# Moving eight rotations, four weight sums and one load within the second block's projection

## The chip, the cores and the metric

The kernel runs on one core of a Trainium2 chip. The metric is the device time in microseconds of one execution, and smaller is better. The profile is one execution of the same program, recorded instruction by instruction. The engines are TensorE (PE, matrix products), VectorE (DVE), ScalarE (ACT), GpSimd (POOL, which here mostly issues DMAs) and SyncE (SP, which issues DMAs only). Each engine works through its own list of instructions in the order in which the program appended them; between engines there are only semaphores.

## The reference

The input x has 2048 rows of 1024 features. Three things are added: x itself, a diagonal state-space layer, and a dense layer, both of the normalised x.

```python
xn = _layernorm(x)
# state-space layer (complex, diagonal, 1024 states)
Lam_bar = exp(dt * Lam);  B_bar = ((Lam_bar - 1) / Lam)[:, None] * Bmat
Bu = einsum("bld,pd->blp", xn, B_bar)
h[t] = Lam_bar * h[t-1] + Bu[t]                     # over 2048 steps
y = 2 * (h @ Cmat.T).real + xn * Dskip
# dense layer, 1024 -> 3584 -> 1024
z = xn @ w1 + b1
return x + y + (z * tanh(softplus(z))) @ w2
```

The result is 2048 x 1024 in bf16.

## The kernel before, in words

**Blocks.** The 2048 rows are worked through in four blocks of 512, blk 0 to 3 in the code. `FAST` is 1, so the code's special cases for `blk == FAST` are those of the second block, and `SPLIT` holds blk 2 and 3. A block has these stages on PE: the dense layer's first product (line 818 in blk 0 and 1), the projection of x by B (line 882), the dense layer's second product and the output product of the states by C (both line 1193, accumulated in the same eight PSUM banks), and then four additions on DVE that put x and the sum together (line 1262, `finish`), each with a store issued by ACT (line 1254).

**The projection.** From blk 1 on the product of x and B isn't made with eight partial products but with seven (a scheme after Strassen), numbered 1 to 7. `project_fast` walks through a written list, `WHOLE` for blk 1, in which each word is one step. The letters a, b, c, d are the four pairs of state tiles, and the digit is the product (`a2`, `c4`). Behind each product `evacuate` copies a bank to SBUF on DVE or ACT (lines 897, 899, 924, 926) or joins it with an earlier copy on DVE (line 907). Products of one pair follow each other in the same banks, so a product may have to wait for a join or a copy: product 4 takes the bank that the join of product 7 reads, for example. The other words are `r` (rotate one state tile by its phase: four DVE operations, lines 848 to 853), `u` (`open_unit`: six matmuls that begin the second dense product in one bank), `v` (`w_scale`: ACT scales a weight group in place, line 1087, and POOL stores three parts of it), `n` (`w_load`: POOL loads a raw weight group in four DMAs, line 1026) and `k0` (take one step from the list `steps` and do it).

**The weight groups.** In blk 2 and 3 the dense layer's first product is made by the same scheme, with letters p, q, s, w, x, y, z. That needs scaled weights and sums of them, prepared once in DRAM (`wsd`) for the seven groups 0 to 6. For one group: load the raw weights into half of the buffer `hb` or into `act`; find their size (for groups 0 to 2: `w_abs`, line 1037 on ACT; `w_row`, two small DMAs `wmd` and `wmx` on POOL; `w_exponent`, lines 1071 to 1078 on DVE); scale; store; then `w_sums`, which puts four steps on the list, each one DVE operation (line 1102) and one POOL store of 256 KB (line 1081). Groups 3, 5 and 0 use the lower half of `hb`, groups 4, 6 and 1 the upper half, group 2 uses `act` 0 to 7. So group 1 can be loaded only when the stores of group 6's sums have left the upper half.

**Order in the second block.** The list of steps for group 5 is made at the last tile of the first dense product, and `WHOLE` takes them with four `k0` between its products. Rotations r0 and r1 stand among the joins of pairs c and d. Behind `project_fast`, ACT takes statistics of the next block's x (`next_stats`) and measures group 0, and the list for group 6 is made. Then the recurrences follow on DVE (`recur`, one state tile each: two scans, line 1158, and four operations). Behind recurrence 0 and 1 two steps of group 6 each are done, then POOL loads group 1, and behind it group 2. Behind recurrence 7 DVE works out the exponents of groups 0 to 2, and ACT scales them. Then DVE adds the skip term to the next block's x (lines 563, 565), forms the differences of x that the fast scheme needs (line 1378), carries the state over, and makes the four output additions. The next block's x is turned by four DMA transposes on SP (line 569).

**Weights on the way.** SP loads all streamed weights into a ring of seven slots (lines 410 and 413), in the order of use, each as soon as its slot has been read.

Of the kernel before, what the change touches and what calls it, by code (L numbers as in the profile page):

```python
# [163 lines left out]
def build_kernel(nc, A_x, A_Lambda_re, A_Lambda_im, A_B_re, A_B_im, A_C_re, A_C_im,  # L164
# [16 lines left out]
    FAST = 1  # L181
    NPL = 12
    SPLIT = range(2, NB)
    GROUPS = ((0, 7), (7, NPL), (NPL, NPL + 8), (NPL + 8, NF))
    HEAD = "a2 a1 b2 b1 a5 b5 a6 b6 a3 b3 a7 b7 c2 d2 a4 b4 c5 c1 r0 d5 d1 r1 c6 c3 d6"
    HEAD1 = "v5 n6 " + HEAD.replace("a4 b4 c5 c1 r0 d5 d1 r1", "a4 b4 k0 c5 c1 k0 r0 d5 d1 k0 r1 k0")
    WHOLE = HEAD1 + " v6 d3 c7 d7 u7 c4 r2 u5 d4 u6 u4 r3 n0 r4 r5 r6 r7"
    LATE = (" a3 b3 a7 b7 c2 d2 a4 b4 c5 c1 d5 d1 c6 c3 d6"
            " d3 c7 w1 d7 w5 w2 c4 d4 w6 r0 x1 x5 x2 w7 w3 r1 x6 w4 y1 y5 y2 x7 x3 r2 y6 x4"
            " z1 z5 g2 z2 y7 y3 z6 y4 u0 z7 u2 z3 u1 z4 u7 g3 r3 r4 r5 r6 r7")  # L190
# [150 lines left out]
    def early(name, shape, dtype, where):  # L341
        b_early.append(Buf(name))
        return nc.alloc_sbuf_tensor_at(name, shape, dtype, offset=base_c + where), b_early[-1]
# [9 lines left out]
    ncs, _ = early("ncs", [P, NR], f32, 10752)  # L353
# [675 lines left out]
    def w_half(i, ci):  # L1029
        kind, t = w_raw(i, ci, 0)  # L1030
        v, b_v = (hb, b_hbf) if kind == "h" else (act, b_actf)
        return v[:, t:t + 4, :].rearrange("p f t -> p (f t)"), b_v[t:t + 4]
# [51 lines left out]
    def w_scale(i):  # L1084
        for ci in range(2):
            t, b_t = w_half(i, ci)
            aop(lambda e, t=t: e.activation(t, t, AF.Copy, scale=wsm(2, i, i + 1)),  # L1087
                reads=b_t + [b_wsm[2][i]], writes=b_t)
        for n, ci, kh in ((1, 0, 0), (2, 0, 1), (4, 1, 1)):
            w_store(i, n, *w_unit(w_raw(i, ci, kh)))  # L1090

    steps = []
# [16 lines left out]
    def project_fast(blk, order, open_unit):  # L1109
        keep = {}  # L1110
        split = order is not WHOLE
        for o in order.split():
            kind, n = o[0], int(o[1:])
            if kind == "r":
                rotate_in(n)
            elif kind == "u":
                open_unit(n)
            elif kind == "g":
                mish(blk, n)
            elif kind == "k":  # L1120
                if steps:
                    steps.pop(0)()
            elif kind == "n":
                w_load(n)
            elif kind == "v":
                w_scale(n)
            elif kind in QUADS:
                w_product(blk, QUADS.index(kind), n)
                w_evacuate(blk, QUADS.index(kind), n, keep)
            else:  # L1130
                product("abcd".index(kind), n)
                evacuate("abcd".index(kind), n, keep, split or kind in "ab")
# [257 lines left out]
    for blk in range(NB):  # L1390

        def side(f):
            if blk:
                at = (8, 10, 12, 15)
                if f in at:
                    ln_skip(blk, at.index(f))
                    if blk >= FAST:
                        sums_x(at.index(f))
                if blk == FAST:
                    if f == 1:  # L1400
                        rows_spread(1)
                    if f == 0:
                        scale_B(0, (1,))
                    if f < 3:
                        scale_B(f + 1)
                    if f in (3, 4, 17, 19):
                        sums_B((3, 4, 17, 19).index(f))
                    if f in (2, 14):
                        w_scale((2, 14).index(f) + 3)
                    if f in (6, 8, 10, 12):  # L1410
                        rows_C(f // 2 + 1)
                    if f == 12:
                        snaps_ready()
                    if f in (10, 19):
                        w_sums((10, 19).index(f) + 3)
                    if f == 15:
                        w_load(5)
                    if f == 27:
                        w_sums(5, True)
                return  # L1420
            if f == 2:
                turn_sines()
            if f == NR:
                aop(lambda e: e.activation(act[:, 0:NR, 0:2 * P], hraw[:, 0:NR, :], AF.Mish),
                    reads=b_hbf[0:4], writes=b_actf[0:NR])
            if f in (19, 27):
                for j in range(4):
                    table(j + (4 if f > 19 else 0))
            if f in (5, 6, 7, 8):
                coefficients(f - 5)  # L1430
            if f in (8, 9, 11, 12):
                ln_skip(0, (8, 9, 11, 12).index(f))
            if f in turns:
                transpose_B(turns.index(f))
            if f >= 26:
                transpose_C(f - 26)
            if f >= 4 * ROWS[0][0] and f % 4 < 2:
                w_most(f // 4, f % 4)
            if f in (23, 25, 26, 27):
                ln_stats_only(1, (23, 25, 26, 27).index(f))  # L1440
            if f == 26:
                w_row(0)

        for f in range(0 if blk in SPLIT else NF):
            first_tile(blk, f)
            side(f)

        near = 0 < blk < NB - 1
        out_stage = tail(blk, n_item[0] + (len(W_ITEMS) if blk in SPLIT else 0))
        open_unit = next(out_stage)  # L1450
        if blk in SPLIT:
            if near:
                for q in range(NQ):
                    load_x(PO, blk + 1, q)
            project_fast(blk, STEPS if near else SEVEN, open_unit)
        elif blk:
            project_fast(blk, WHOLE, open_unit)
        else:
            project_in()
        if near and blk not in SPLIT:  # L1460
            for q in range(NQ):
                next_stats(blk + 1, q)
            w_abs(0)
            w_sums(6, True)
        for j in range(NJ):
            if blk == 0 and j == NJ - 1:
                rows_scale(0)
            recur(blk, j)
            if blk == FAST and j < 2:
                for _ in range(2):  # L1470
                    steps.pop(0)()
                if j == 1:
                    w_load(1)
            if near and j == (5 if blk in SPLIT else 1):
                next_root()
                for q in range(NQ):
                    next_scale(blk + 1, q)
            if blk in SPLIT:
                if j == 1:
                    next(out_stage)  # L1480
                if near and j == 1:
                    for q in range(NQ):
                        next_stats(blk + 1, q)
                if near and j == 5:
                    for q in range(NQ):
                        transpose_dma(q)
                continue
            if blk:
                if j == 1:
                    next(out_stage)  # L1490
                    w_load(2)
                    w_abs(1)
                    w_abs(2)
                    w_row(1)
                if j == 7:
                    w_exponent(1)
                    for i in (0, 1, 2):
                        w_scale(i)
                continue
            if j == 0:  # L1500
                ln_root()
                w_exponent(0)
                for q in range(NQ):
                    ln_scale(1, q)
                next(out_stage)
                for i in range(NHS):
                    rows_load(i)
            scale_C(j)
            for i in {4: (0, 1, 2), 5: (3, 4, 5, 6), 6: (7, 8, 9, 10), 7: range(11, 16)}.get(j, ()):
                rows_size(i)  # L1510
        if near:
            for q in range(NQ):
                ln_skip(blk + 1, q)
            for n in range(4):
                sums_x(n, VE)
        if blk < NB - 1:
            carry()
        if blk == FAST:
            for i in (0, 1, 2):
                w_sums(i, True)  # L1520
        if blk == FAST - 1:
            w_load(3)
            rows_scale(1)
            vop(lambda e: e.tensor_tensor(qi[:], qi[:], c("ss").unsqueeze(1).to_broadcast([P, 2, NJ]), op=ALU.mult),
                reads=[b_qi] + b_ss, writes=[b_qi])
            rows_spread(0)
            scale_B(0, (0,))
            for j in range(4):
                rows_C(j)
            w_load(4)  # L1530
        for _ in out_stage:
            pass
# [36 lines left out]
```

## Time and profile before

| what | value |
|---|---|
| median of 3 runs | 608.08 us (605.46 to 609.31) |
| the profiled execution's own time | 609.85 us |
| its span, first to last instruction | 608.6 us |
| mean granted TensorE clock | 0.997 |
| DVE, ACT, POOL busy | 475.4, 278.5, 122.8 us |
| first dense product and projection of blk 1 | 162 to 210 us, 210 to 238 us |
| last output product of blk 1 ends | 311.8 us |
| the same of blk 2 | 462.8 us |

A line of the profile names the engine, the line of the kernel, what is written and what is read (`ps<-xnT,ring` writes PSUM from x and a ring slot), and the shape. In a timeline the first two numbers are the start and the length in us; `x16` joins sixteen equal instructions, and brackets tell how long the engine sat idle before and what ended that. In the view of waits the numbers are the total, the count and the longest. In the chain each line is a stretch of time and who filled it; the chain is followed back from the last instruction, each time to what released it. Two matmuls of 512 columns start 0.219 us apart at full clock, two of 256 columns 0.109 us; the durations shown are longer, since matmuls overlap. The share of the DMA engines can come out a little over 1.

### The profile page before, as it was taken

What the parts mean: (1) busy time and instruction counts of PE and PEld (TensorE: products, weight loads), DVE (VectorE), ACT (ScalarE), POOL (GpSimd) and SP (SyncE); (2) the same over time, 40 slices, a digit from 0 to 9 for tenths busy, and PEclk for the clock granted to TensorE, in tenths of its full rate; (3) what the DMA queues carried; (4) which work ended last, traced back from release to release, by engine and by line L of the source; (5) the groups of instructions that cost most, each with busy time, mean ns of one, the idle gap of its engine ahead of it and who ended that gap; (6) DMA issues with size and microseconds to landing.
All of it is one profiled execution on the core that took longest, in us unless ns stands there. A gap on an engine that the chain in (4) does not pass through costs nothing.

```text
span 608.6 us, 9262 instructions
## 1 busy us (share of the span) xinstructions
PE 595.7 (98%) x3541; PEld 348.8 (57%) x3583; DVE 475.4 (78%) x748; ACT 278.5 (46%) x367; POOL 122.8 (20%) x162
## 2 busy tenths in 40 slices
PE   8999999999999999999979999999999999999998
PEld 7644444444444585444448888544446888744444
DVE  6998899999789579998186876699943577689923
ACT  4749605489488526834077417470304615620000
POOL 2899200221338333040034100000000000000000
PEclk9999999999999999999989999999999999999999
DMA  9999997992999955699969817554667705764421
GB/s 237 312 236 274 203 195 215 255 356 59 280 357 339 329 179 173 221 236 186 301 247 401 323 53 251 197 193 141 185 193 250 282 6 171 245 207 144 167 71 69
DMA packets 109670, 132.95 MB, mean 218 GB/s; under 512 B 54346, under 2 KB 69322, under 8 KB 109626
## 3 DMA queue, kind: packets, MB, share of 16 engines
q1 hardware_dynamic: 97168, 95.77, 54.4%
q0 software_dynamic: 8768, 28.26, 14.5%
q10 hardware_dynamic: 3690, 8.34, 3.9%
q8 instruction: 28, 0.46, 0.3%
q14 instruction: 16, 0.13, 0.1%
HBM read 99.04 MB, written 21.24 MB: 198 GB/s over the span
## 4 chain that ended last, share of the span: by engine, by line
PE 78%; DVE 9%; DMA 5%; issue 5%; ACT 2%; POOL 1%; SPq 1%; ACTq 0%; DVEq 0%; POOLq 0%
PE ps L1193 37%; PE ps L818 14%; PE ps L952 11%; PE ps L882 10%; PE ps L1139 5%; DMA ring<-in_B_w_dram 2%; DVE mt L848 2%; ACT snaps L972 2%; DMA wmd<-cs 1%; PE ps L638 1%; DVE xx L1262 1%; DVE hT L907 1%; DVE hT L1158 1%; DMA wmx<-wmd 1%; DMA wsd<-hb 1%
## 5 line engine op out<-in xcount | busy, mean ns | idle before, releaser
L1193 PE MATMUL ps<-ring,act 128*128 128x512 bf16 x876 | 194.2, 379 | 2.1 <-DMA ring<-in_B_w_dram 1.1
L1193 PEld LDWEIGHTS ps<-ring,act 128*128 128x128 bf16 x896 | 87.4, 98 | 105.1 <-DMA ring<-in_B_w_dram 2.4
L818 PE MATMUL ps<-xnT,ring 128*128 128x512 bf16 x383 | 84.3, 379 | 0.5
L1193 PE MATMUL ps<-ring,hT 128*128 128x512 bf16 x369 | 81.6, 379 | 0.5
L972 ACT ACTIVATE snaps<-ps,par,cs 128x256 f32<-128x256 f32 x80 | 43.2, 562 | 84.6 <-PE ps L952 49.6
L818 PEld LDWEIGHTS ps<-xnT,ring 128*128 128x128 bf16 x392 | 38.4, 98 | 46.0
L1193 PEld LDWEIGHTS ps<-ring,hT 128*128 128x128 bf16 x378 | 37.0, 98 | 44.6
L1158 DVE TENSOR_TENSOR_SCAN hT<-cs,qi,hT 128x512 bf16<-128x512 f32 x48 | 58.9, 1267 | 0.0
L952 PE MATMUL ps<-TT,ring 128*128 128x256 f16 x448 | 56.6, 275 | 1.0 <-ACT snaps L972 1.0
L989 DVE SCALAR_TENSOR_TENSOR act<-ps,cs,snaps 128x512 bf16<-128x512 f32 x42 | 31.4, 750 | 32.3 <-PE ps L952 29.0
L952 PEld LDWEIGHTS ps<-TT,ring 128*128 128x128 f16 (+1 forms) x448 | 44.0, 98 | 7.7 <-issue 1.5
L952 PE MATMUL ps<-xnT,ring 128*128 128x256 bf16 x336 | 43.8, 276 | 3.1 <-DVE xx L1262 3.1
L826 ACT ACTIVATE act<-ps,par 128x512 bf16<-128x512 f32 (+1 forms) x56 | 34.1, 664 | 19.8 <-PE ps L818 18.0
L1163 DVE TENSOR_TENSOR mt<-hT,tab 128x1024 bf16<-128x1024 bf16 x64 | 41.4, 687 | 1.1
L952 PEld LDWEIGHTS ps<-xnT,ring 128*128 128x128 bf16 (+1 forms) x336 | 33.3, 99 | 8.5 <-issue 3.6
L1081 POOL DMA_DIRECT2D wsd<-hb x42 | 22.8, 544 | 62.1 <-DVE hb L1102 39.8
L841 ACT ACTIVATE act<-act 128x4096 bf16<-128x4096 bf16 (+2 forms) x8 | 25.5, 3188 | 19.7 <-DVE act L975 19.7
L1262 DVE TENSOR_TENSOR xx<-ps,xx 128x1024 bf16<-128x1024 f32 (+1 forms) x16 | 18.5, 1186 | 18.7 <-PE ps L1193 18.6
L848 DVE TENSOR_TENSOR mt<-hT,tab 128x1024 bf16<-128x1024 f16 x48 | 30.9, 685 | 0.4
L897 DVE COPY snaps<-ps 128x512 f32<-128x512 f32 x30 | 19.9, 685 | 12.9 <-PE ps L882 12.8
L1087 ACT ACTIVATE hb<-hb,cs 128x2048 bf16<-128x2048 bf16 x12 | 23.2, 1993 | 13.8 <-DVE cs L1076 13.8
L907 DVE TENSOR_TENSOR hT<-ps,snaps 128x512 f16<-128x512 f32 x36 | 24.4, 689 | 5.6 <-PE ps L882 3.7
(178 smaller groups left out, 804.6 us busy)
## 6 DMA issues: line engine op xcount, KB each, us to landing
ring<-in_B_w_dram SPq DMA_DIRECT2D x84, 512.0 KB, 4.6
ring<-wsd SPq DMA_DIRECT2D x98, 256.0 KB, 4.2
ring<-ctd SPq DMA_DIRECT2D x24, 512.0 KB, 3.4
wsd<-hb POOLq DMA_DIRECT2D x42, 256.0 KB, 4.8
hb<-in_B_w_dram POOLq DMA_DIRECT2D x24, 256.0 KB, 5.2
ctd<-act ACTq DMA_DIRECT2D x8, 512.0 KB, 5.7
out_dram<-xx ACTq DMA_DIRECT2D x15, 256.0 KB, 3.7
xx<-in_A_x_dram POOLq DMA_DIRECT2D x12, 256.0 KB, 6.7
```

The costliest lines, as they stand in the source:

```text
L818: PE.mm(lambda e, k=k, w=w: e.matmul(ps[:, bank, :], lhsT=w, rhs=xnT[:, k, :], start=k == 0, stop=k == NK - 1), reads=[b_ring[s]] + b_xnT, ...
L826: aop(lambda e: e.activation(at[0][:, ts], ps[:, bank, ts], AF.Mish, bias=b1(f)), reads=[b_ps[bank], b_par], writes=[at[1]])
L848: vop(lambda e, s=s: e.tensor_tensor(mt[:, s, :, :], hT16[:, :, j, :], tab[:, s, j, :].unsqueeze(1).to_broadcast([P, 2, TB]), op=ALU.mult) ...
L882: PE.mm(lambda e, w=w, x=x, o=o, begin=begin, end=end: e.matmul(ps[:, bank, o:o + TH], lhsT=w, rhs=x, start=opens and begin, stop=end, ski ...
L907: vop(lambda e: e.tensor_tensor(dst, bank(b), src, op=ALU.add), reads=[b_ps[b], b_src], writes=b_hT[ci][j0:j0 + 2])
L952: PE.mm(lambda e, w=w, x=x, o=o, begin=begin, end=end: e.matmul(ps[:, bank, o:o + TH], lhsT=w, rhs=x, start=opens and begin, stop=end, ski ...
L972: aop(lambda e, o=o, p=p, j=j: e.activation(o, p, AF.Identity, scale=ig, bias=b1(f0 + j)), reads=[b_ps[b], b_par, b_ig], writes=b_dst)
L989: vop(lambda e: e.scalar_tensor_tensor(out=dst, in0=bank(b), scalar=ig, in1=src, op0=ALU.mult, op1=ALU.add), reads=[b_ps[b], b_snap[k], b_ ...
L1139: PE.mm(lambda e, j=j, ci=ci, k=k, bank=bank: e.matmul(ps[:, bank + ci, :], lhsT=BT[:, ci, j, k, :], rhs=xnT[:, k, :], start=k == 0, stop= ...
L1158: vop(lambda e, ci=ci, init=init: e.tensor_tensor_scan(out=hT[:, ci, j, :], data0=cj("r", j).to_broadcast([P, TB]), data1=hT[:, ci, j, :], ...
L1163: vop(lambda e, s=s: e.tensor_tensor(mt[:, s, :, :], hT[:, :, j, :], tab[:, s, j, :].unsqueeze(1).to_broadcast([P, 2, TB]), op=ALU.mult), ...
L1193: PE.mm(lambda e: e.matmul(ps[:, u, :], lhsT=lhsT, rhs=rhs, start=st_, stop=last), reads=reads, writes=[b_ps[u]], first=st_, last=last, te ...
```

## The change

The first part concerns the list `WHOLE`. All eight rotations now stand behind the last joins (`c7`, `d7`): r0 to r2 between the remaining products and `u` steps, r3 to r7 at the end. The four `k0` for group 5 stay among the products. Four more `k0` stand behind r4 and r5, and they do the sums of group 6. A new word `n1` loads group 1 right behind them, ahead of r6 and r7.

The second part makes the lists of steps elsewhere: the word `v` now scales a group and puts its sums on the list at once. So the calls for group 5 (at f == 27) and group 6 (behind `w_abs(0)`) go, and so do the steps and the load of group 1 behind recurrence 0 and 1. `v` stands in `WHOLE` alone. `HEAD` and `HEAD1` were used only for `WHOLE`.

```diff
-    HEAD = "a2 a1 b2 b1 a5 b5 a6 b6 a3 b3 a7 b7 c2 d2 a4 b4 c5 c1 r0 d5 d1 r1 c6 c3 d6"
-    HEAD1 = "v5 n6 " + HEAD.replace("a4 b4 c5 c1 r0 d5 d1 r1", "a4 b4 k0 c5 c1 k0 r0 d5 d1 k0 r1 k0")
-    WHOLE = HEAD1 + " v6 d3 c7 d7 u7 c4 r2 u5 d4 u6 u4 r3 n0 r4 r5 r6 r7"
+    WHOLE = ("v5 n6 a2 a1 b2 b1 a5 b5 a6 b6 a3 b3 a7 b7 c2 d2 a4 b4 k0 c5 c1 k0 d5 d1 k0 c6 c3 k0 d6 v6 d3 c7 d7 u7 r0 c4 u5 r1"
+             " d4 u6 r2 u4 n0 r3 r4 k0 k0 r5 k0 k0 n1 r6 r7")
...
             elif kind == "v":
                 w_scale(n)
+                w_sums(n, True)
...
-                    if f == 27:
-                        w_sums(5, True)
...
             w_abs(0)
-            w_sums(6, True)
...
             recur(blk, j)
-            if blk == FAST and j < 2:
-                for _ in range(2):
-                    steps.pop(0)()
-                if j == 1:
-                    w_load(1)
```

## The prediction

> **What bounds the kernel now.** I read the page's busy shares first, then PE's waits, then PE's timeline where those waits lie, then the chain that ended last. The blocks are the code's blk 0 to 3; the change stands in blk 1.
>
> ```profile
> PE 595.7 (98%) x3541; PEld 348.8 (57%) x3583; DVE 475.4 (78%) x748; ACT 278.5 (46%) x367; POOL 122.8 (20%) x162
> ```
>
> PE is busy for 595.7 of 608.6 us, and the change takes no matmul away. All that can be won or lost is PE's idle time (12.9 us in the whole span) and time in which PE runs below its clock. The view of waits, for PE, names the idle time that matters:
>
> ```profile
> PE ps L952 <- DVE xx L1262: 3.1, 1, 3.1
> PE ps L882 <- DVE hT L907: 1.3, 1, 1.3
> PE ps L952 <- ACT snaps L972: 1.0, 2, 0.8
> ```
>
> The 1.3 us lie in blk 1's projection, the 3.1 us and 0.8 us where blk 1 ends and blk 2 starts. First the projection, in PE's timeline:
>
> ```profile
> 232.62 1.24 PE L1193 MATMUL ps<-ring,act 128*128 128x512 bf16 x5
> 235.18 1.05 PE L882 MATMUL ps<-TT,BT 128*128 128x256 f16 x8 [1.31 <-DVE hT L907]
> ```
>
> Product c4 needs the bank that the join of c7 reads, and DVE makes the last four joins only at 233.24 to 235.71, behind the rotations r0 (227.44) and r1 (230.64). Now the boundary of blk 1 and 2, and the same place of blk 2 and 3:
>
> ```profile
> 285.71 26.06 PE L1193 MATMUL ps<-ring,hT 128*128 128x512 bf16 x117
> 314.86 1.03 PE L952 MATMUL ps<-xnT,ring 128*128 128x256 bf16 x8 [3.09 <-DVE xx L1262]
> 315.73 1.84 PE L952 MATMUL ps<-TT,ring 128*128 128x256 f16 x8
> 317.36 2.82 PE L952 MATMUL ps<-xnT,ring 128*128 128x256 bf16 x16
> ...
> 324.43 1.91 PE L952 MATMUL ps<-TT,ring 128*128 128x256 f16 x16 [0.76 <-ACT snaps L972]
> ```
>
> ```profile
> 454.82 7.93 PE L1193 MATMUL ps<-ring,hT 128*128 128x512 bf16 x35
> ...
> 469.97 1.91 PE L952 MATMUL ps<-TT,ring 128*128 128x256 f16 x16 [0.23 <-ACT snaps L972]
> ```
>
> Between the last output matmul (285.71 + 26.06 = 311.77) and the matmuls at 324.43 lie 64 matmuls of 256 columns, and they take 12.66 us. The same 64 in the later boundary take 469.97 - 462.75 = 7.22 us. The difference, 5.44 us, is the wait of 3.09, a slow stretch behind it (8 matmuls in 1.63 us from 315.73, 16 in 2.66 from 317.36, where 0.87 and 1.75 are usual: 1.67 us; the granted clock of 316 to 320 is 0.60), and 0.53 more of waiting for ACT, whose evacuations start late for the same reason. The chain tells why DVE is late:
>
> ```profile
> 260.37 4.52 DMA wsd<-hb
> ...
> 265.46 2.23 POOL hb L1026 x3
> 267.70 2.95 POOL act L1026 x4
> ...
> 290.54 7.12 DMA wmd<-cs
> ...
> 297.94 4.57 DMA wmx<-wmd
> 302.53 0.68 DVE cs L1071
> ```
>
> The last store of the seventh weight group's sums lets POOL load group 1 and behind it group 2 (L1026); ACT measures both (L1037); the small transfers wmd and wmx follow, and DVE, idle since 287.1, waits 15.3 us for wmx. It then has 11.0 us of work (302.53 to 313.5: exponents, skip, differences of x, carry) before the four output additions L1262. ACT's timeline shows which load is late:
>
> ```profile
> 260.28 4.63 ACT L556 ACTIVATE xn<-xx,ln 128x1024 bf16<-128x1024 bf16 x4 [4.44 <-DVE ln L552]
> 275.99 3.62 ACT L1037 ACTIVATE CT<-hb 128x4096 bf16<-128x4096 bf16 x1 [11.07 <-DMA hb<-in_B_w_dram]
> 286.54 3.62 ACT L1037 ACTIVATE CT<-act 128x4096 bf16<-128x4096 bf16 x1 [6.84 <-DMA act<-in_B_w_dram]
> ```
>
> **The change, part by part.** *Rotations behind the joins.* DVE's operations stay the same. I lay the joins out again, each about 0.18 us behind PE or at once behind ACT, as in the trace: d1 at 228.0, c3 at 229.2, d3 at 230.8, c7 at 231.7 to 232.4, d7 at 232.6 to 233.2, with the four sums of group 5 in the gaps. PE could start c4 when u7 ends, at 233.87, so c7's join is 1.5 us early and the wait of 1.31 goes. What is late next for PE is u4, which takes c4's bank after ACT's copy: ACT ends the seventh group's scaling at about 234.4 and copies c4 by 235.5, PE wants u4 at 238.1. **Gain 1.31.** DVE pays: its rotations start only at 233.2, and the gaps before that stay idle. Eight rotations of 2.10 (six took 235.64 to 248.24) and four sums (two pairs of 1.33) end at 233.2 + 16.8 + 2.7 = 252.7, against 248.24 + 2.7 = 250.9 before. All recurrences come 1.75 us later. That is covered: the first is at 257, PE asks for it near 281.
>
> *Sums of the seventh group between rotations.* Four DVE operations and four POOL stores move ahead of r5 to r7 and two recurrences. Five rotations from 233.2 end at 243.7, two sums at 245.0, r5 at 247.1, two sums at 248.5; before, the last ended at 259.96. So they are 11.5 us earlier. Their inputs, scaled on ACT by 234.6 and stored by 238.8, are ready. POOL's order is unchanged (loads of group 0, these stores, loads of group 1, of group 2), and nothing else stands behind the waiting loads.
>
> *Group 1's load directly behind.* Its four loads started at 262.73 to 266.95, group 2's at 267.69 to 269.90, released by the stores; 11.5 us earlier they run from 251.2 to 259. Group 2's target, eight tiles of act, is last read by PE at about 249. Landing took 3.5 to 16.6 us here. At the shortest end both are there when ACT comes free, 264.91 + 1.75 = 266.7; at 9.0 and 16.6 us group 2 lands at 275.1. I take the short side, since these loads now come before the four transposes (from 267.41), which fill the DMA engines (shares of 1.08 and 1.09, at only 209 and 113 GB/s, in 268 to 280). ACT then measures at 266.7 and 270.5, done by 274.3 (278.9 at worst); wmd and wmx as before, 7.4 + 4.57: landed at 286.3 (290.9). DVE leaves its last recurrence at 287.1 + 1.75 = 288.9, so the exponents start at 288.9 to 290.9 and not at 302.53. The differences of x, 7.6 us behind, need the transposes, the last of which landed at 291.8. DVE is ready for the additions at 299.9 to 301.9. PE ends the first pair of banks at 302.6 (the last at 310.46, three times 2.62 before it), so DVE waits for PE, as in the later boundary. **Gain 5.44**, less whatever the weight loads then cost.
>
> *The weight loads.* With the stall gone, PE asks for blk 2's scaled weights 6.75 us sooner, and from 312 to 345 the DMA engines are full (368 to 414 GB/s). Issued from 310.1 on: 33 ring loads, 12 stores of sums, 6 scaled stores, 4 loads of x, 4 outputs, each 0.262 MB, 15.5 MB or 38.4 us at 403 GB/s, which ends at 348.5 as the trace does. The six scaled stores and about two outputs now fall earlier: 13.4 MB, 33.2 us from 308.8, ending at 342.0, 6.3 sooner. That keeps pace with PE within 0.4 us, and the tightest weight unit (issued 320.26, landed 326.5, used 332.28) had 5.8 us. Cost 0; the other end is the whole gain of 5.44.
>
> The Trainium skill, "DMA: Bandwidth & Descriptors", Specifications, gives a core's HBM limit as some 358 GB/s, which would speak against the change: an estimate from it is 13.4 MB in 37.4 us, 4.2 longer, 605.6 us in all. The trace disagrees: 332 to 336 moved 414 GB/s.
>
> **Sum.** 1.31 + 5.44 = 6.75. The profiled execution took 609.85 us (span 608.6), so it would be 603.1. The median shown is 608.08, and I forecast **601.4**. The two waits left in blk 2, 1.1 us for ring loads near 383 and 0.33 near 343, I leave as they are; they could go (600.0).
>
> The slow matmuls fit the Trainium skill, "TensorE: Matmul & The Clock Gate", part 1, by which the array's clock halves after an idle window of about 3.4 us. Here 3.09 us were enough. By that rule a wait left at 1 or 2 us would cost no clock, so a partial success keeps the 1.67 us too.
>
> **Rivals.** (1) *The transfers bind the start of blk 2.* For it: full engines for 33 us, and PE asking sooner. Against: 2.1 MB leave that stretch, and blk 3 starts without stalls while its engines are as full (1.03 to 1.05 share, 464 to 476). Price: if nothing left the stretch, the loads would run 1.31 earlier for a PE that is 6.75 earlier, so 5.44 at the far end (606.8) and nothing where the 5.8 us of margin cover it; the middle is 604.1. (2) *The chain does not get shorter*, because group 2's load lands no sooner among transposes. Then only c4 is won: 606.8. It takes a landing of 27 us; the longest was 16.6. (3) *Slower:* the nine scaled stores, pulled to 292 to 304, hold up the last output weights (ring<-ctd, issued 288.7 to 289.9, landed in up to 8.0). PE wants the first of them at 298.2, so it waits once a landing takes over 9.5 us, and the sum turns slower at 14.6 (5.1 of waiting and 1.67 of clock). Such a load took 16.3 us from 270.42; with the stores' 2.4 MB in front (5.9 us at 403 GB/s) it is 22.2, PE waits 12.7, and 14.4 lost against 6.75 won gives 615.7. Against it: those stores are issued after these loads. (4) *The change does not do what it says*: the sums find their tiles still being stored, and nothing moves: 608.
>
> **Numbers.** Forecast 0.73, (1) 0.11, (2) 0.06, (3) 0.07, (4) 0.03. The forecast's own range is 599.5 to 603.5 (waits left or gone, and the 3.9 us over which the three runs scatter). The range takes in the far end of (1), which is also (2), 606.8, and starts at 599.0, the waits gone and a run 1 us to the low side; it leaves out (3), (4) and tails of the forecast, under 2 in 10. One per cent is 6.1 us, about what a measurement here tells from no change, and the forecast lies just beyond it (602.0), so 0.21 of its chance and all of (1), (2) and (4) fall within: faster 0.52, same 0.41, slower 0.07.
>
> **What would show it.** Right: no wait of L882 for L907; sums L1102 of the seventh group by 249; L1037 at about 267 and 271; no long DVE wait for wmx; L1262 waiting for PE four times; 64 matmuls at the boundary in 7.2 us; no clock of 0.6. Wrong: PE waits for ring<-wsd or ring<-ctd, or L1037 for its load past 279.

## The result and the profile after

The changed kernel takes 602.99 us (median of 9 runs, 601.72 to 604.22) against 608.6 us (9 runs, 605.46 to 611.32). The ratio is 0.9908, with a 95% interval of 0.9885 to 0.9931. Its profiled execution took 603.15 us, with a span of 601.9 us, against 609.85 and 608.6 us. Most lines of the kernel have moved up by one: L882 of before is L881 of after, L952 is L951, L1037 is L1036. Lines 1139 to 1400 kept their numbers.

PE's waits in the profile after (total, count, longest):

```profile
PE ps L628 <- DMA ring<-in_B_w_dram: 2.0, 1, 2.0
PE ps L590 <- DVE filler L422: 1.0, 1, 1.0
PE ps L1193 <- DMA ring<-in_B_w_dram: 0.7, 1, 0.7
PE ps L951 <- ACT snaps L971: 0.5, 2, 0.2
PE ps L881 <- DVE snaps L896: 0.3, 1, 0.3
```

The wait for a join (1.3 us) and the wait for the output additions (3.1 us) are gone. The 2.0 us at the top are at the very start of the program, for the first weights; the same wait was 0.7 us in the profile before. The change has no part in it: the run with the load at its old place, below, turns out to be the same program as the changed kernel, and there it is 0.8. Here are the two places in PE's timeline of after (start, length, what, and the idle time before it):

```profile
233.18 1.24 PE L1193 MATMUL ps<-ring,act 128*128 128x512 bf16 x5
234.26 1.04 PE L881 MATMUL ps<-TT,BT 128*128 128x256 f16 x8
...
283.06 27.79 PE L1193 MATMUL ps<-ring,hT 128*128 128x512 bf16 x125
310.68 1.04 PE L951 MATMUL ps<-xnT,ring 128*128 128x256 bf16 x8
...
318.06 1.91 PE L951 MATMUL ps<-TT,ring 128*128 128x256 f16 x16 [0.23 <-ACT snaps L971]
```

Product c4 follows u7 without a gap. From the last output matmul (283.06 + 27.79 = 310.85) to the mark at 318.06 it is 7.21 us and no longer 12.66, and no matmul there is slow. The span's 6.7 us can be laid out along PE's timelines, before against after: PE enters blk 1's projection at 209.70 and 210.26 (0.56 lost at the start of the program), leaves it at 238.23 and 237.30 (1.49 won), is level from there to the end of the output product (311.77 and 310.85), wins 5.45 up to the mark (324.43 and 318.06), and 0.40 more in the ring waits near 380. ACT's timeline of after shows the loads in time:

```profile
262.42 4.63 ACT L555 ACTIVATE xn<-xx,ln 128x1024 bf16<-128x1024 bf16 x4 [7.50 <-DVE ln L551]
266.96 3.60 ACT L1036 ACTIVATE CT<-hb 128x4096 bf16<-128x4096 bf16 x1
...
270.74 3.62 ACT L1036 ACTIVATE CT<-act 128x4096 bf16<-128x4096 bf16 x1
```

Both measurements now start as soon as ACT is free, where before they waited 11.07 and 6.84 us for their loads. And DVE, in its timeline of after, never waits for wmx:

```profile
289.26 0.66 DVE L1070 TENSOR_REDUCE cs<-wmx 128x3 f32<-128x384 f32 x1
...
303.11 1.23 DVE L1262 TENSOR_TENSOR xx<-ps,xx 128x1024 bf16<-128x1024 f32 x1 [3.17 <-PE ps L1193]
```

The exponents start at 289.26 and not at 302.53, and the output additions wait for PE, four times.

### The profile page after: what moved, and what is told of

Read it like the earlier page. It is cut to its first block, busy times and chain, and to the rows that moved or that the text cites. A ratio compares the mean times of both kernels' runs of the same rounds, so it can differ in the third digit from the quotient of the medians.

```text
span 601.9 us, 9263 instructions
## 1 busy us (share of the span) xinstructions
PE 593.0 (99%) x3541; PEld 347.7 (58%) x3583; DVE 476.9 (79%) x748; ACT 278.4 (46%) x367; POOL 123.0 (20%) x162
## 4 chain that ended last, share of the span: by engine, by line
PE 93%; DMA 2%; DVE 2%; ACT 2%; issue 1%; SPq 0%; ACTq 0%; DVEq 0%
PE ps L1193 50%; PE ps L817 14%; PE ps L881 11%; PE ps L951 11%; PE ps L1139 5%; DMA ring<-in_B_w_dram 2%; ACT snaps L971 2%; PE ps L628 1%; PE ps L637 1%; DVE act L1101 0%; DVE xx L1262 0%; DVE snaps L896 0%; DVE hT L906 0%; PE ps L1219 0%; DVE act L974 0%
## 5 line engine op out<-in xcount | busy, mean ns | idle before, releaser
L951 PE MATMUL ps<-TT,ring 128*128 128x256 f16 x448 | 55.8, 273 | 0.5 <-ACT snaps L971 0.5
L951 PEld LDWEIGHTS ps<-TT,ring 128*128 128x128 f16 (+1 forms) x448 | 43.7, 98 | 6.9 <-issue 1.0
L825 ACT ACTIVATE act<-ps,par 128x512 bf16<-128x512 f32 (+1 forms) x56 | 34.0, 665 | 19.6 <-PE ps L817 17.9
L951 PE MATMUL ps<-xnT,ring 128*128 128x256 bf16 x336 | 42.9, 273 | 0.0
L1262 DVE TENSOR_TENSOR xx<-ps,xx 128x1024 bf16<-128x1024 f32 (+1 forms) x16 | 18.8, 1189 | 24.5 <-PE ps L1193 24.4
L951 PEld LDWEIGHTS ps<-xnT,ring 128*128 128x128 bf16 (+1 forms) x336 | 32.9, 98 | 4.7
```

Source lines behind the costliest of these rows:

```text
L825: aop(lambda e: e.activation(at[0][:, ts], ps[:, bank, ts], AF.Mish, bias=b1(f)), reads=[b_ps[bank], b_par], writes=[at[1]])
L951: PE.mm(lambda e, w=w, x=x, o=o, begin=begin, end=end: e.matmul(ps[:, bank, o:o + TH], lhsT=w, rhs=x, start=opens and begin, stop=end, ski ...
```

## The experiments

Each edit is made to the kernel before unless "changed kernel" is said. "Boundary" is the place where blk 1 ends and blk 2 starts, and the wait at the boundary is PE's wait there for the output additions.

### Each part alone, the sums a little later, the load where it was

**The rotations alone.** `WHOLE` is that of the change without its last four `k0` and without `n1`; the sums of group 6 and the load of group 1 stay behind recurrences 0 and 1.

```diff
-    WHOLE = HEAD1 + " v6 d3 c7 d7 u7 c4 r2 u5 d4 u6 u4 r3 n0 r4 r5 r6 r7"
+    WHOLE = ("v5 n6 a2 ... a4 b4 k0 c5 c1 k0 d5 d1 k0 c6 c3 k0 d6 v6 d3 c7 d7 u7 r0 c4 u5 r1"
+             " d4 u6 r2 u4 n0 r3 r4 r5 r6 r7")
```

> The rotations stand behind the last joins, but the sums of group 6 and the load of group 1 stay behind recurrences 0 and 1. My theory: the end of blk 1 is set by DVE's chain (sums, loads, measuring, wmd, wmx, exponents, output additions), so PE's gain of 1.3 to 1.5 us in front of c4 is waited away again, and since the rotations start later on DVE, the last sum ends at 262.1 and not 259.96, the exponents start near 304.7 and the matmuls marked at 324.43 come near 326.5: span 610.7, slower than before by about 2 us. Rival: each part of the change is worth its own wait; then this one wins 1.5 us, span 607.1.

Measured: 603.73 us (6 runs), ratio 0.9909 (0.9882 to 0.9936), span 601.8. Both expectations were wrong. The sums did come later, the last at 261.1, and group 1's load with them (from 263.8). But while ACT's first measurement started 1.0 us later than before (275.99), its second started 5.7 us earlier (286.54), and with it the exponents 7.7 us earlier (302.53). ACT's and DVE's timelines of this run:

```profile
277.02 3.62 ACT L1036 ACTIVATE CT<-hb 128x4096 bf16<-128x4096 bf16 x1 [10.97 <-DMA hb<-in_B_w_dram]
...
280.82 3.62 ACT L1036 ACTIVATE CT<-act 128x4096 bf16<-128x4096 bf16 x1
```

```profile
294.79 0.67 DVE L1070 TENSOR_REDUCE cs<-wmx 128x3 f32<-128x384 f32 x1 [6.46 <-DMA wmx<-wmd]
```

Group 2's last load took 9.9 us from issue to landing and not 16.6, so ACT went from one measurement straight to the other. DVE was in time for PE (no wait at the boundary). PE waited 0.4 us for blk 2's scaled weights (`ring<-wsd`, near 322), the only profile with such a wait there, so the margin of those loads is not large. My theory had carried the landing times of one profile over as if they were fixed. They were the variable.

**The sums and the load alone.** The change, with r0 and r1 back among the joins and r2, r3 where they were:

```diff
-... k0 c5 c1 k0 d5 d1 k0 c6 c3 k0 d6 v6 d3 c7 d7 u7 r0 c4 u5 r1 d4 u6 r2 u4 n0 r3 r4 k0 k0 r5 k0 k0 n1 r6 r7
+... k0 c5 c1 k0 r0 d5 d1 k0 r1 k0 c6 c3 d6 v6 d3 c7 d7 u7 c4 r2 u5 d4 u6 u4 r3 n0 r4 k0 k0 r5 k0 k0 n1 r6 r7
```

> The sums of group 6 and the load of group 1 stand early, but r0 and r1 stay among the joins. My theory: the wait in front of c4 stays (1.3 us), the boundary is as short as in the changed kernel (7.2 us from the last output matmul to the mark): span 603.2, ratio 0.991 of before. Rival: the rotations' move is needed for the boundary too, since it makes DVE's order; then the boundary stays long and the span is near 608.

Measured: 604.14 us (6 runs), ratio 0.9914 (0.9891 to 0.9936), span 602.2. The boundary is as short as in the changed kernel, and the wait in front of c4 is back, as this line of PE's waits says:

```profile
PE ps L881 <- DVE hT L906: 1.3, 1, 1.3
```

So either part alone removes the boundary's wait, and the two don't add up. What only the rotations' move brings is the 1.3 us.

**The sums behind r7**, in the changed kernel:

```diff
-             " d4 u6 r2 u4 n0 r3 r4 k0 k0 r5 k0 k0 n1 r6 r7")
+             " d4 u6 r2 u4 n0 r3 r4 r5 r6 r7 k0 k0 k0 k0 n1")
```

> As the changed kernel, but the four sums of group 6 and the load of group 1 stand behind r7: the last sum ends near 253 and not 249, the loads start 4 us later. My theory: ACT comes free at 267 anyway and DVE is busy until 289.3, while wmx landed at 284.0, and DVE then waits 3.2 us more for PE: the 4 us are covered, PE has no new wait, span 601.9 as in the changed kernel (within 0.5). Rival: what is won goes in proportion to how much earlier the sums are; 4 of 11 us lost is some 2 us, span 604.

Measured: 602.83 us (6 runs), ratio 0.9894 (0.9871 to 0.9917), span 602.1. The last sum ended at 252.7, the loads started at 257.6, wmx landed at 287.7, DVE took it up at 288.85 without a wait, and PE had no new wait. Four microseconds of lateness cost nothing.

**The load of group 1 at its old place**, in the changed kernel: `n1` goes, and `w_load(1)` stands behind recurrence 1 again.

> As the changed kernel, but the load of group 1 is written behind recurrence 1 as before; the sums stay early. My theory: on POOL nothing stands between, so its four loads wait for nothing but the stores, and start at 253.9 as in the changed kernel; same time, span 601.9 (within 0.5), ratio 0.989 to 0.993. Rival: the load's place in the list counts; it then starts near 262, and with it part of the gain goes, span 604 to 607.

Measured: 602.68 us (6 runs), ratio 0.9891 (0.9867 to 0.9915), span 601.2. The lists of instructions and waits of all five engines are the same as the changed kernel's: on POOL the load's neighbours are the stores before it and group 2's load behind it in either program. So `n1` in itself does nothing. The load comes early because the stores do. The run also serves as the changed kernel once more. Timed side by side, before took 609.29 us, the sums alone 604.14 and this one 602.68: 5.15 us for the boundary and 1.46 for the joins.

### What makes the loads late

**Before, once more, and the rotations alone once more.**

> The kernel before, unchanged, profiled and timed once more. The rotations alone won as much as the whole change, with the loads of groups 1 and 2 no earlier (from 263.8), but landed in 9.1 and 9.9 us and not in 9.0 and 16.6; the first two transposes took 7.4 and 12.8 us there and 16.4 and 16.0 before. New theory: how long these loads and the transposes hold each other up differs from execution to execution, and with it the wait at the boundary; a second profile of before then shows other landings (group 2 between 9 and 17 us), wmx between 293 and 305, and a span that follows it: 605 with no wait at the boundary, up to 610. Rival: it is fixed by the order of the issues; then it again shows 16 us, wmx at 302.5 and a wait of 3.1 us, span 608.6 within 0.5.

> The rotations alone, profiled once more. If the meeting of loads and transposes differs from execution to execution: group 2's last load lands anywhere between 9 and 17 us after its issue, span 601 to 607. If the order of the issues fixes it: again 10 us and a span of 601.8 within 0.5.

Measured: before 609.08 us (12 runs, 607.1 to 612.78; ratio to itself 1.0003, 0.9978 to 1.0029), span 611.5; the rotations alone 602.05 us (one run), span 600.8. The second profile of before is worse than the first. PE's waits and DVE's wait in it:

```profile
PE ps L952 <- DVE xx L1262: 5.6, 1, 5.6
PE ps L882 <- DVE hT L907: 1.3, 1, 1.3
```

```profile
DVE cs L1071 <- DMA wmx<-wmd: 17.8, 1, 17.8
```

Its first two transposes took 17.7 and 18.8 us and group 2's last load 18.9. In the rotations' second profile they took 6.2, 11.5 and 8.5 us. So neither expectation held in full: sizes differ by some 2 us between the two profiles of a kernel, but in both pairs it was the kernel that decided whether the loads landed late and PE waited.

**The transposes later.** Nothing of the sums, loads or rotations is touched; only the tiles of the second dense product behind which the transposes are issued:

```diff
-            f1 = 17 if blk else 9
+            f1 = 21 if blk else 9
```

> The kernel before, with the four transposes of the next block's x four tiles later in the second dense product (from tile 21 on and not 17), some 7 us later, from 274.4; sums, loads and rotations as before. If the boundary's wait comes from the meeting of the loads and the transposes: group 2 lands in under 10 us, by 280, wmx by 296, no DVE wait of PE at the boundary, only the 1.3 us in front of c4 stays, span 603.3. If the late sums as such make the wait: the loads start at 262.7 as before, wmx stays near 302, span 608.

Measured: 604.05 us (8 runs, 603.94 to 604.84), ratio 0.9923 (0.9896 to 0.9951), span 602.8. Group 2 landed at 279.7, wmx at 292.8, and the boundary's wait was gone. The sums were as late as before (the last ended at 259.75, in before at 259.96). This settles that their lateness alone doesn't make the wait.

**The transposes earlier, and half as much later** (`f1 = 15` and `f1 = 19`):

> The kernel before, with the four transposes two tiles earlier in the second dense product (from tile 15 on and not 17), 3.5 us; the first then goes out near 264, as soon as its rows are normalised. Both profiles of before show the first two transposes at 16 to 19 us, both of the rotations alone 6.3 to 12.8; there PE, and with it the transposes, came about 2.5 us sooner against the loads of groups 1 and 2. If that distance decides: first transpose under 8 us, group 2 landed by 282, wmx by 297, no wait at the boundary, only the 1.3 us in front of c4, span 603.3. If the rotations' place as such decides: as before, wmx at 302 to 305, span 608 to 611.

> The kernel before, with the transposes from tile 19 on, 3.5 us later, half of what the run from tile 21 had (there the first transpose took 7.3 us and the wait at the boundary was gone). If the meeting with group 2's loads (267.7 to 269.9) decides, they have landed for the most part when the first transpose goes out at 270.9: first transpose 8 to 12 us, wmx between 293 and 298, no wait or one under 1 us, span 603 to 604.5. Rival: only a distance of 7 us is enough; wmx at 302, span 608.

Measured: 604.24 us (6 runs), ratio 0.9915 (0.9888 to 0.9942), span 604.7; and 604.23 us (6 runs), ratio 0.9912 (0.9884 to 0.9940), span 602.9. Neither has a wait at the boundary. (The span of 604.7 holds 0.9 us of a wait at the end of blk 0 and 1.5 us for the first weights, both long before the transposes.) The first transpose took 6.6 and 8.9 us, wmx landed at 294.6 and 292.4. Moving the transposes by 3.5 us helps in either direction.

**Without group 2's load** (`w_load(2)` is left out):

> The kernel before without the load of group 2: what is measured, scaled and summed for that group is what lies in act 0 to 7, so this part of the weights is not computed. Transposes, sums, rotations and group 1's load are as before. If group 2's load holds up the transposes and is held up by them: the first transpose lands within 8 us, ACT measures group 1 at about 272 and then group 2's place at once, done by 280, wmx by 292, no wait at the boundary, span 603.3. If the transposes are slow by themselves at that place: still 14 to 18 us; wmx is early all the same, so the transposes' own times decide this one.

Measured: 604.71 us (4 runs), ratio 0.9918 (0.9887 to 0.9949), span 603.5. The first two transposes took 9.2 and 7.9 us (I had said under 8) and not 16 to 19; ACT measured at 275.8 and 279.6, wmx landed at 292.9, and PE didn't wait. I had expected the measurement of group 1 at 272: its last load landed no faster without group 2's (8.7 us, in before 9.0). So the slow meeting needs group 2's load. Whether it needs group 1's as well is not shown: that was in flight in all three profiles with the wait at the boundary, and in no run does group 2's load meet the first transpose without it.

**Both cures together.** The rotations alone, and the transposes from tile 19 on:

> The rotations alone (as in the first run) together with the transposes 3.5 us later (from tile 19 on). Each of the two by itself took the wait at the boundary away. In before the first transpose went out 0.3 and 0.4 us ahead of group 2's first load; with the rotations alone 3.4 and 3.6 us ahead, with earlier transposes 3.9 ahead, with later ones 3.1 and 6.6 us behind. Here both moves cancel, and the first transpose goes out within 0.5 us of group 2's first load again. If that meeting makes the wait: first transpose 13 to 18 us, wmx at 300 or later, PE waits for the output additions again, span 606 to 610, though each half was worth over 5 us. If rotations behind the joins or transposes later help by themselves: no wait, span 601.8.

Measured: 610.44 us (12 runs), ratio 1.0010 (0.9991 to 1.0029), span 608.9. Two edits of which each wins 5 us win nothing together, as expected from the distance of the issues (the first transpose took 18.3 us; I had said 13 to 18). PE's waits, DVE's wait, and the landing times of the first two transposes (line 568) in this run:

```profile
PE ps L951 <- DVE xx L1261: 5.7, 1, 5.7
```

```profile
DVE cs L1070 <- DMA wmx<-wmd: 14.9, 1, 14.9
```

```profile
DMA to landing us min/median/max: 17.3/17.8/18.3
```

The same landing times of the first two of the rotations alone were 7.4 and 12.8 us. For comparison, two pairs of lines: the loads of groups 1 and 2, then the transposes issued from 262 to 285, first in before, then in the transposes half as much later:

```profile
DMA to landing us min/median/max: 3.5/10.2/16.6
DMA to landing us min/median/max: 6.9/16.0/16.4
```

```profile
DMA to landing us min/median/max: 3.6/6.1/7.9
DMA to landing us min/median/max: 5.0/6.5/8.9
```

The wait in front of c4 (1.3 us in before) is absent here, so the rotations' move did its part, and the boundary's wait, 5.7 us against 3.1 in the first profile of before, ate it.

The windows show the meeting itself. The last two numbers of a row are the busy share of the DMA engines and GB/s. Before, then these two cures together, then the transposes half as much later:

```profile
273.00:276.00 3.00, 2.95 (x15) 1.35 (x14) 3.00 (x4) 0.01 (x1) 0.00 (x0) 1.00 0.93 77
276.00:279.00 3.00, 3.00 (x15) 1.37 (x14) 2.93 (x6) 3.00 (x1) 0.00 (x0) 1.00 1.20 131
279.00:282.00 3.00, 3.00 (x15) 1.37 (x14) 2.93 (x5) 0.70 (x2) 0.00 (x0) 1.00 0.86 138
```

```profile
276.00:279.00 3.00, 3.00 (x16) 1.37 (x14) 2.97 (x4) 2.12 (x1) 0.00 (x0) 1.00 0.66 40
279.00:282.00 3.00, 3.00 (x16) 1.35 (x14) 2.97 (x5) 1.59 (x2) 0.00 (x0) 1.00 1.12 98
282.00:285.00 3.00, 3.00 (x16) 1.35 (x15) 2.93 (x6) 0.00 (x0) 0.00 (x0) 1.00 1.06 109
```

```profile
273.00:276.00 3.00, 3.00 (x15) 1.37 (x14) 2.96 (x5) 2.02 (x1) 0.00 (x0) 1.00 1.02 314
276.00:279.00 3.00, 3.00 (x15) 1.37 (x14) 2.96 (x5) 2.91 (x3) 0.00 (x0) 1.00 1.30 190
279.00:282.00 3.00, 3.00 (x15) 1.37 (x14) 2.93 (x5) 2.49 (x2) 0.22 (x1) 1.00 1.07 348
```

Where the two meet, the engines move 40 to 138 GB/s for 9 us, at busy shares of 0.66 to 1.20. In the third run, with shares of 1.02 to 1.30, it is 190 to 348. The view of the DMA queues tells one thing more. These are the lines of POOL's queue, which carries the loads, from 273 to 282 (packets, MB, share of the 16 engines), in before and in the transposes half as much later:

```profile
q0 software_dynamic: 239, 0.78, 60.0%
```

```profile
q0 software_dynamic: 193, 0.60, 23.3%
```

An estimate from them: 60.0% of 16 engines for 9 us, over 239 packets, is 0.36 us for a packet, against 0.17 us in the second. The same working, on 9 us of each profile, gives 0.35 and 0.48 us in the other two with the wait (from 273 and from 276), and 0.17 to 0.23 us while these loads ran in those without the wait. So in the meeting a packet of a load, of much the same size (some 3.1 to 3.4 KB), took about twice as long or more.

**Group 2 loaded twice**, in the changed kernel (a second `w_load(2)` behind the first):

> The changed kernel, with group 2's load made twice, one right behind the other (1 MB more, issued from 259.9 to 262.9, into the transposes' start). Theory: the second load and the transposes hold each other up as before (first transposes over 8 us, against 4.4 to 5.7 in the changed kernel), wmx lands some 4 to 8 us later, at 288 to 292, and PE does not wait, since DVE has 3.2 us left: span 601.9 to 602.5. Rival: the changed kernel has no room left, and each us shows: span 606 or more.

Measured: 603.15 us (5 runs), ratio 0.9907 (0.9873 to 0.9941), span 602.8. (The 0.9 us over the changed kernel's span are waits of the second dense product for its ring loads, 1.6 us in all against 0.7; at the boundary PE's timeline is level with the changed kernel's, 318.07 against 318.06.) The second load started later than I had said, at 268.4, since it must not overtake the first, which landed at 268.1. It went out 1.9 us behind the first transpose, and the first two transposes took 6.0 and 8.2 us, so the slow meeting that I had expected (over 8 us) did not come about. wmx landed at 291.4, DVE waited 2.0 us for it and then still 1.0 for PE, and PE had no wait at the boundary. The changed kernel has room there.

### The runs side by side

"Ahead" (negative: behind) is by how much the first transpose was issued before group 2's first load in the profiled execution; times in us.

| kernel | first transpose ahead by | it took | group 2's last load took | DVE waited for wmx | PE waited for the output additions | ratio |
|---|---|---|---|---|---|---|
| before | 0.3 | 16.4 | 16.6 | 15.3 | 3.1 | 1 |
| before again | 0.4 | 17.7 | 18.9 | 17.8 | 5.6 | 1.0003 |
| rotations alone, transposes half later | 0.0 | 18.3 | 17.9 | 14.9 | 5.7 | 1.0010 |
| rotations alone | 3.4 | 7.4 | 9.9 | 6.5 | 0 | 0.9909 |
| rotations alone, again | 3.6 | 6.2 | 8.5 | 4.6 | 0 | (602.05 us) |
| transposes earlier | 3.9 | 6.6 | 9.5 | 6.2 | 0 | 0.9915 |
| transposes half later | -3.1 | 8.9 | 7.9 | 5.4 | 0 | 0.9912 |
| sums behind r7 | -5.1 | 8.8 | 9.8 | 0 | 0 | 0.9894 |
| transposes later | -6.6 | 7.3 | 10.0 | 5.8 | 0 | 0.9923 |
| changed kernel | -9.6 | 5.7 | 9.7 | 0 | 0 | 0.9908 |
| load at its old place | -9.4 | 5.9 | 8.9 | 0 | 0 | 0.9891 |
| sums and load alone | -11.3 | 6.1 | 7.9 | 0 | 0 | 0.9914 |

The table looks at the first transpose alone. In the three profiles that have it 3.4 to 3.9 us ahead, the second transpose went out within 0.4 us of group 2's first load, and it took 11.5 to 12.8 us, against 16.0 to 18.8 in the profiles with the wait and 4.4 to 7.5 in those with the first transpose behind. So the two met there too, in a milder form: the loads still landed in 8.5 to 9.9 us, and that was soon enough for PE. The distance sorts these profiles, but it is not shown to be the mechanism, and none of them lies between 0.4 and 3.1 us.

## Why the prediction was right, and where it was not

**The join in front of c4: right.** Predicted 1.31; the wait is gone, PE's timeline wins 1.49 there (the idle time leaves out some 0.2 us by which matmuls overlap), and the medians of kernels timed side by side put it at 1.46. The joins came where they were laid out: c7 at 232.29 with PE 0.56 later (predicted 231.7), and c4 didn't wait.

**The sums and the load: right in their dates.** The last sum ended at 248.99 (predicted 248.5), group 1's load ran from 253.9 and group 2's last from 259.1 (251.2 to 259), ACT measured at 266.96 and 270.74 (266.7 and 270.5), wmx landed at 284.0 (286.3), the exponents started at 289.26 (288.9), and the 64 matmuls took 7.21 us (7.22).

**The boundary: right in its size for the profiled pair, 5.45 against 5.44, but only half right in its cause.** (The three parts that the prediction names, 3.09, 1.67 and 0.53, add up to 5.29; the rest is about the overlap of matmuls just mentioned.) The step was "the last store of the seventh weight group's sums lets POOL load group 1 ... ACT's timeline shows which load is late". That chain is in the trace, and pulling its start forward by 11 us does remove the wait (the sums alone). But what made the load late was not its start. It was a landing of 16.6 us, against some 8 to 10 us in most other runs, which it had because it met the transposes; with an ordinary landing, the late sums did no harm at all. I had those rows in hand ("Landing took 3.5 to 16.6 us here", "the four transposes (from 267.41), which fill the DMA engines", 209 and 113 GB/s) and used them only to choose the short end for the changed kernel. I never asked whether the long end was itself the cause. That is why the expectation for the rotations alone failed by 9 us of span (610.7 against 601.8).

**The weight loads of blk 2: right.** PE waits for ring<-wsd nowhere in the profile after, although it was only counted, and shown by no run, that 2.1 MB would leave that stretch. The limit of the Trainium skill's "DMA: Bandwidth & Descriptors", Specifications, weighed there, had given 605.6 us; the run came out below it, and 330 to 340 moved 406 GB/s in the profile after, against 402 and 409 in the two halves of that stretch before. Two small slips in the working change nothing: from 348.5 to 342.0 it is 6.5 us and not 6.3, and 608.08 less 6.75 is 601.3 and not 601.4.

**From the profile to the median.** I took 6.75 us off a median of 608.08 and forecast 601.4; the medians of 9 runs differ by 5.6. The gain was read from one execution of before, and that one is 1.25 us above its own median of 9. A kernel with the meeting scatters (before 605.5 to 611.3, and 607.7 to 612.3 with both cures), most without it less (0.7 us in the run with the load at its old place, 2.5 in the changed kernel, but 4.0 in the rotations alone). Part of the scatter is the clock. Of the 59 executions of before that were timed beside the experiments, 30 had a mean granted clock of 1.000 and a median of 607.8 us, and 29 one of 0.994 to 0.997 and a median of 610.8; with both cures all twelve lay below 1.000, and in no kernel without the wait did one. So the slow matmuls, 1.67 us of the sum, came about in only half of the executions of before, as far as the mean clock tells. The term of 5.44 is one draw; the medians of kernels timed side by side give 5.15, and those of the result give 5.6 less 1.46, some 4.1. The two ring waits near 383, left as they were, shrank from 1.1 to 0.7. That the profiled execution, 603.15 us, met the 603.1 of the sum is partly luck: 0.56 us lost at the start of the program were made up by those 0.40 and by the 0.18 more at the join.

**The rivals.** (1), the transfers bind, did not happen. (2) did not happen either: it asked for a landing of 27 us, and group 2's last load took 9.7. (3), the output weights held up, did not happen: the last three ring<-ctd landed in 3.4 to 5.5 us. (4) neither.

## What to carry to other kernels

When a chain of waits runs through a DMA, ask first whether that DMA's time to landing is the usual one for its size; if it took twice as long as its neighbours, look for what was in flight with it and move either of the two, before anything upstream is hurried. Moving the other transfer by 3.5 us was worth as much here as moving four sums by 11. And such a meeting is a matter of a few microseconds: two edits that each avoid it can bring it back together, so a change that wins this way should be tried again after every later shift.

## What the runs showed of the hardware

In these runs DMA transposes on SP's queue and plain 256 KB loads on POOL's slowed each other down, and how much depended on a few microseconds. With the first transpose issued 0.0 to 0.4 us ahead of group 2's four loads (and behind group 1's), it took 16.4 to 18.3 us in all three profiles, and the last of the loads 16.6 to 18.9; for some 9 us the DMA engines were busy and moved 36 to 187 GB/s, and a packet of the loads took 0.35 to 0.48 us (the estimate above) where 0.17 to 0.23 is usual. With the first transpose 3.1 us or more behind, no transpose took over 8.9 us. With it 3.4 to 3.9 us ahead, it took 6.2 to 7.4 us itself, the next two still 10.2 to 12.8, and the loads at most 9.9. With group 2's second load 1.9 us behind, and group 1's landed, it was 6.0. Group 1's load was in flight in all of the cases with the wait and some of those without, so it is not enough by itself, as the run without group 2's load shows (9.2 us). Why so few microseconds decide stays open: no view of the profile tells how an engine orders its packets. The Trainium skill, "DMA: Bandwidth & Descriptors", Queues, rings and completion order, says that an engine takes turns between its queues packet by packet. That would let the packets of a transpose and of a load wait for each other whenever both are in flight, at a distance of 3 us too, so by itself it doesn't explain the difference.

The clock: behind a wait of 3.1 us, and of 5.6 and 5.7, eight matmuls of 256 columns took 1.63 to 1.71 us where 0.87 is usual, in each of the three profiles that had the wait and in no other at this place.
